# Decode attention on one core: how the first half of the first K is loaded

## The chip, the cores and the metric

The kernel runs on one core of one Trainium2 chip. The metric is the device time of the launch in microseconds (us). Each kernel was timed against the kernel before on the same chip.

## The reference, cut to what matters

One query per head attends to 8192 keys, for 16 heads of width 256:

```python
B, H, Sq, Sk, D = 1, 16, 1, 8192, 256          # q, k, v in bf16
scores = einsum("bhqd,bhkd->bhqk", q, k) * D ** -0.5
out = einsum("bhqk,bhkd->bhqd", softmax(scores), v)
```

K and V are 64 MiB each and each byte is used once. 134.2 MB have to be read from device memory (134.23 in the trace of before); there is little arithmetic per byte.

## The kernel before

A head's K is laid out as 128 partitions of 64 keys ("columns"), 32 KB per partition, and comes in two halves of 32 columns. A half is normally one load of 2 MB: 128 rows of 16 KB. In the traces each row of a load is one packet: before has 9344 data packets, as many as rows (512 of 2 KB, 512 of 4 KB, 640 of 8 KB, 7680 of 16 KB). About 16 packets are under way at a time (exactly 16 for 278 of 318 us), and the page counts 16 DMA engines; what is given per engine below is a sum over packets divided by 16. There are four buffers for halves of K and four for halves of V. The half of K with number n is used by VectorE (columns 0 to 23, one fused multiply-and-sum per column, 0.346 us from one start to the next: 12 of them from 9.30 to 13.45 us in before) and by TensorE (columns 24 to 31). When both are done with it, its buffer takes half n + 4.

All loads are issued in one order by one queue: K halves 0, 1, 2, 3; then K4, V0, K5, V1 and so on. K4 has to wait until K0 has been used, and nothing behind it in this order is issued earlier (V0 followed K4 at 14.26 us in before).

```python
def cuts(kind, n):                       # widths of the loads of one half, in columns
    if kind == "k" and n == 0:
        return FIRST_CUT                 # (4, 4, 8, 16): rows of 2, 2, 4 and 8 KB
    if kind == "v" and n == NIT - 1:
        return LAST_CUT
    if kind == "v" and n in (NIT - 3, NIT - 2):
        return BEFORE_CUT
    return (HALF,)                       # 32 columns: rows of 16 KB
...
for kind, h, x in items:                 # the loads, in the order above
    ...
    if n >= slots:
        waits = [f"{kind}free{n - slots}"] + ([f"ktfree{n - slots}"] if kind == "k" else [])
    for i, wd in enumerate(cuts(kind, n)):
        plan.op("sp", lambda e, ...: e.dma_start(
            b[:, at * D : (at + wd) * D], cols(t, h, c + at, c + at + wd)), ...)
        at += wd
...
# VectorE: one instruction per column, waiting for the load that holds this column
plan.op("dve", lambda e, ...: e.tensor_tensor_reduce(...), name,
        [f"qbc{h}", ring] + landed("k", n, c, c + 1))
```

The cut of K0 into four loads lets VectorE start on the first four columns early (at 4.09 us, see below).

## Time and profile before

| | |
|---|---|
| time, median of the first 3 runs | 324.47 us (324.17 to 325.11) |
| span of the profiled run | 323.3 us |
| data read | 134.2 MB, 415 GB/s over the span |
| VectorE busy | 275.6 us (85%) |
| DMA share | 9 tenths or more in 38 of 40 slices |

Two lines of the page of the kernel before: the DMA share in tenths and the GB/s moved, in 40 equal slices of the span (8.1 us each).

```profile
DMA  7999999999999999999999999999999999999993
GB/s 230 431 438 423 424 430 432 426 424 424 431 432 428 424 432 428 432 426 426 434 430 428 424 428 432 430 430 421 428 432 430 430 423 434 426 428 430 416 417 142
```

From 1.72 us, where the first data packet starts, to 320.05 us, where the last one ends, some data packet is under way at all times but 2 ns. Apart from the last slice, which holds the tail, only the first is slow. The next table, by stages of the kernel before, has the stretch in us, its length, the busy time of PE, PEld, DVE, ACT and POOL with instruction counts, the granted clock, the DMA share and GB/s.

```profile
2.00:8.00 6.00, 1.34 (x6) 0.46 (x6) 2.85 (x16) 1.59 (x6) 0.54 (x5) 1.00 0.91 298
8.00:20.00 12.00, 7.59 (x76) 5.48 (x76) 10.37 (x59) 5.99 (x10) 0.00 (x0) 1.00 1.02 436
50.00:300.00 250.00, 179.67 (x1794) 125.72 (x1791) 228.12 (x1315) 73.69 (x144) 0.00 (x0) 0.87 1.01 428
```

From 2 to 8 us the engines are 91% busy and yet move 298 GB/s; later they move 428. So the share of busy time doesn't say here that the stream is at its rate: read the two columns together.

VectorE's first instruction, and the two later ones in the first 16 us that waited for K (timeline of the kernel before: start, length, engine, line, operation, and in brackets the idle time before it with what ended it):

```profile
4.09 0.42 DVE L359 CUSTOM_DVE_ANT_0 prod<-Kb,qbc 128x256 bf16<-128x256 bf16 x1 [4.09 <-ACT qbc L421]
...
8.06 0.43 DVE L359 CUSTOM_DVE_ANT_0 prod<-Kb,qbc 128x256 bf16<-128x256 bf16 x1 [1.11 <-DMA Kb<-in_k_dram]
...
15.44 0.42 DVE L359 CUSTOM_DVE_ANT_0 prod<-Kb,qbc 128x256 bf16<-128x256 bf16 x1 [1.57 <-DMA Kb<-in_k_dram]
```

The third is the start of the second half of K. VectorE's last instruction on K0 ended at 13.86 us, and the issuing queue then sent K4:

```profile
13.89 0.33 SPq L318 DMA_DIRECT2D Kb<-in_k_dram  x1
```

Last, who VectorE waited for in the whole run (total us, times, longest), and the end of the chain of waits (start, length, what):

```profile
DVE prod L359 <- DMA Kb<-in_k_dram: 22.9, 20, 1.6
```

```profile
306.89 12.36 DMA Vb<-in_v_dram
319.29 1.92 PE acc L604 x16
321.24 0.46 ACT o L618
```

The run ends as the last V loads land, and 4 us after that. So the time is set by when the DMA stream finishes: its start, its rate and any gap in it.

### The profile page before, as it was taken

What the parts mean: (1) busy time and instruction counts of PE and PEld (TensorE: products, weight loads), DVE (VectorE), ACT (ScalarE), POOL (GpSimd) and SP (SyncE); (2) the same over time, 40 slices, a digit from 0 to 9 for tenths busy, and PEclk for the clock granted to TensorE, in tenths of its full rate; (3) what the DMA queues carried; (4) which work ended last, traced back from release to release, by engine and by line L of the source; (5) the groups of instructions that cost most, each with busy time, mean ns of one, the idle gap of its engine ahead of it and who ended that gap; (6) DMA issues with size and microseconds to landing.
All of it is one profiled execution on the core that took longest, in us unless ns stands there. A gap on an engine that the chain in (4) does not pass through costs nothing.

```text
span 323.3 us, 6446 instructions
## 1 busy us (share of the span) xinstructions
PE 223.0 (69%) x2166; PEld 155.7 (48%) x2166; DVE 275.6 (85%) x1586; ACT 94.1 (29%) x185; POOL 1.9 (1%) x12
## 2 busy tenths in 40 slices
PE   1557068783968767685876658676667956858897
PEld 0335045562656545453554535454444644535574
DVE  3899999999999999988889988889888889888600
ACT  3455032422141423323213242312422223232010
POOL 2000000000000000000000000000000000000000
PEclk9999999998697979789778987977887797898799
DMA  7999999999999999999999999999999999999993
GB/s 230 431 438 423 424 430 432 426 424 424 431 432 428 424 432 428 432 426 426 434 430 428 424 428 432 430 430 421 428 432 430 430 423 434 426 428 430 416 417 142
DMA packets 10558, 134.36 MB, mean 416 GB/s; under 512 B 1186, under 2 KB 1203, under 8 KB 2228
## 3 DMA queue, kind: packets, MB, share of 16 engines
q1 hardware_dynamic: 10512, 134.22, 98.2%
q8 instruction: 5, 0.08, 0.1%
q14 instruction: 5, 0.04, 0.0%
q10 hardware_dynamic: 36, 0.02, 0.0%
HBM read 134.23 MB, written 0.01 MB: 415 GB/s over the span
## 4 chain that ended last, share of the span: by engine, by line
DMA 56%; DVE 38%; PE 2%; issue 2%; SPq 1%; DVEq 0%; ACT 0%
DMA Kb<-in_k_dram 41%; DVE prod L359 36%; DMA Vb<-in_v_dram 15%; PE acc L604 2%; DVE S L359 1%; SPq L318 1%; DVE g L331 0%; DVE recip L340 0%; ACT o L618 0%; DVE m L378 0%; DVEq L150 0%; DVEq L147 0%; DVEq L144 0%
## 5 line engine op out<-in xcount | busy, mean ns | idle before, releaser
L359 DVE CUSTOM_DVE_ANT_0 prod<-Kb,qbc 128x256 bf16<-128x256 bf16 x768 | 269.4, 411 | 28.9 <-DMA Kb<-in_k_dram 22.9
L604 PE MATMUL acc<-Vb,E 128*1 128x256 bf16 x1024 | 148.2, 315 | 9.4 <-DMA Vb<-in_v_dram 9.0
L604 PEld LDWEIGHTS acc<-Vb,E 128*1 128x1 bf16 x1024 | 96.5, 96 | 53.5 <-DMA Vb<-in_v_dram 10.7
L499 ACT ACTIVATE KT<-tp 128x1024 bf16<-128x1024 bf16 x64 | 62.0, 1021 | 117.2 <-PE tp L490 117.2
L359 DVE DVE_READ_ACCUMULATOR2_ANT S<- 128x1 f32 x768 | 56.9, 74 | 0.0
L490 PE MATMUL tp<-identb,Kb 128*128 128x128 bf16 x512 | 38.2, 234 | 9.0 <-DMA Kb<-in_k_dram 8.9
L490 PEld LDWEIGHTS tp<-identb,Kb 128*128 128x128 bf16 x512 | 32.3, 105 | 17.1 <-issue 14.4
L516 PE MATMUL spe<-qcur,KT 128*128 128x1 bf16 x512 | 20.6, 165 | 19.6 <-ACT KT L499 19.6
L555 PE MATMUL misc<-g,ones_row 1*128 1x1 f32 x32 | 7.1, 287 | 36.7 <-DVE g L331 36.7
L516 PEld LDWEIGHTS spe<-qcur,KT 128*128 128x128 bf16 x512 | 16.4, 99 | 24.5 <-ACT KT L499 24.3
L618 ACT ACTIVATE o<-acc,recip 1x256 bf16<-1x256 f32 x16 | 7.4, 464 | 71.2 <-PE acc L604 71.2
L555 PEld LDWEIGHTS misc<-g,ones_row 1*128 1x128 f32 x32 | 5.7, 221 | 39.7 <-DVE g L331 39.5
L544 PE MATMUL misc<-ident,m 128*1 128x128 f32 x34 | 7.1, 293 | 15.6 <-DVE m L378 15.6
L544 PEld LDWEIGHTS misc<-ident,m 128*1 128x1 f32 x34 | 1.9, 82 | 19.2 <-DVE m L378 18.8
L562 ACT ACTIVATE negb<-misc 128x1 f32<-128x1 f32 x16 | 2.7, 171 | 27.1 <-PE misc L555 27.1
L331 DVE TENSOR_REDUCE g<-misc 1x1 f32<-1x128 f32 x17 | 4.7, 274 | 5.2 <-PE misc L544 5.2
L584 PE MATMUL misc<-ones_col,lsum 128*1 128x1 f32 x34 | 3.2, 164 | 3.7 <-ACT E L569 3.7
L569 ACT ACTIVATE E<-S,negb 128x64 bf16<-128x64 f32 x16 | 5.6, 348 | 0.7 <-ACT negb L562 0.2
L340 DVE RECIPROCAL recip<-misc 1x1 f32<-1x1 f32 x17 | 2.6, 151 | 3.7 <-PE misc L584 3.7
L438 ACT ACTIVATE qbc<-qb 128x256 bf16<-128x256 bf16 x14 | 5.6, 400 | 0.0
L529 ACT ACTIVATE S<-spe 128x16 f32<-128x16 f32 x16 | 2.9, 183 | 7.2 <-PE spe L516 7.2
L412 PE MATMUL tp<-q,identb 16*128 16x256 bf16 x15 | 4.2, 406 | 1.0 <-ACT qb L421 0.5
(25 smaller groups left out, 21.8 us busy)
## 6 DMA issues: line engine op xcount, KB each, us to landing
Kb<-in_k_dram SPq DMA_DIRECT2D x31, 2048.0 KB, 28.6
Vb<-in_v_dram SPq DMA_DIRECT2D x29, 2048.0 KB, 32.5
Vb<-in_v_dram SPq DMA_DIRECT2D x4, 1024.0 KB, 21.1
Vb<-in_v_dram SPq DMA_DIRECT2D x3, 512.0 KB, 11.6
Kb<-in_k_dram SPq DMA_DIRECT2D x1, 1024.0 KB, 8.3
Kb<-in_k_dram SPq DMA_DIRECT2D x2, 256.0 KB, 3.0
Kb<-in_k_dram SPq DMA_DIRECT2D x1, 512.0 KB, 6.3
Vb<-in_v_dram SPq DMA_DIRECT2D x2, 256.0 KB, 12.6
```

The costliest lines, as they stand in the source:

```text
L331: lambda e: e.tensor_reduce(g[0:1, s : s + 1], misc[s][0:1, MT0 : MT0 + P], AX.X, ALU.max),
L359: lambda e, slot=slot, c=c, col=col, h=h, r=(ttr - 1) % PROD: e.tensor_tensor_reduce(out=prod[:, r * D : (r + 1) * D], in0=Kb[slot][:, c * ...
L412: lambda e, i=i, src=src: e.matmul(bank[:, i * D : (i + 1) * D], lhsT=src[0], rhs=src[1], start=True, stop=True),
L438: lambda e: e.activation(out=qbc[:, s * D : (s + 1) * D], in_=qb[:, (h - 2) * D : (h - 1) * D], func=ACT.Copy),
L490: lambda e, c=c, hf=hf, i=(b * NH + hf) * P, view=view: e.transpose(view[:, i : i + P], Kb[slot][:, c * D + hf * P : c * D + (hf + 1) * P] ...
L499: lambda e, gn=gn, view=view: e.activation(out=KT[gn % KT_SLOTS][:, :], in_=view[:, 0 : GROUP * D], func=ACT.Copy),
L516: lambda e, b=b, hf=hf, oc=oc, gn=gn: e.matmul(spe[sl(h)][:, oc : oc + 1], lhsT=KT[gn % KT_SLOTS][:, (b * NH + hf) * P : (b * NH + hf + 1) ...
L544: lambda e: e.matmul(misc[s][0:1, MT0 : MT0 + P], lhsT=m[:, s : s + 1], rhs=ident[:, :], start=True, stop=True),
L555: lambda e: e.matmul(misc[s][:, BC0 : BC0 + 1], lhsT=ones_row[0:1, :], rhs=g[0:1, s : s + 1], start=True, stop=True),
L569: lambda e: e.activation(out=E[:, s * J : (s + 1) * J], in_=S[:, s * J : (s + 1) * J], func=ACT.Exp, bias=negb[:, h : h + 1], scale=SCALE, ...
L604: lambda e, c=c, col=col: e.matmul(a[0:1, 0:D], lhsT=E[:, col : col + 1], rhs=Vb[slot][:, c * D : (c + 1) * D], start=(x == 0 and c == 0), ...
L618: lambda e: e.activation(out=o[0:1, h * D : (h + 1) * D], in_=acc[s][0:1, 0:D], func=ACT.Copy, scale=recip[0:1, s : s + 1],),
```

## The change

The intent is to make the first load like all others: no short rows and three loads fewer, at the price of a later start of VectorE. The diff is one line:

```diff
-FIRST_CUT = (4, 4, 8, 16)
+FIRST_CUT = (32,)
```

The compute instructions stay the same, apart from three semaphores that VectorE and TensorE no longer wait for; the issuing queue has three loads fewer.

## The prediction

> **What bounds the kernel now.** The DMA stream. On the page the DMA share is 9 from the second slice to the last but one; the table by stages gives 428 GB/s from 50 to 300 us. 134.2 MB at that rate are 314 of the span's 323.3 us; the rest is start-up, a slow stretch at the beginning, and 4 us of tail after the last load of V. VectorE is second (275.6 us, 85%): a half of K costs it 24 x 0.346 + 0.3 = 8.6 us, while the DMA needs 9.8 us for a half of K and one of V. The groups show only 22.9 us of VectorE waits for K.
>
> **The slow stretch.** From 2 to 8 us, when the four small loads run, the DMA moves 298 GB/s although its engines are 91% busy; from 8 to 20 us it moves 436. The missing 130 GB/s over 6 us are 0.8 MB, or 1.8 us at full rate. [...] Some of the loss may be the ramp of a cold stream, which stays.
>
> **What changes.** Removed: three DMA issues, the short rows, and three semaphores that VectorE tests again at every fourth half of K. Added: VectorE can't start on the first 8 columns at 4.09 us; it waits for 2 MB. With data from about 1.9 us on, 4.9 us for 2.1 MB at full rate, and about 2 us from last byte to landing (now 4.2 MB are through at 13.4 us and the second half of K is usable at 15.4), I estimate VectorE's first instruction at 8.5 to 9 us. Without its present waits (1.1 us at 8 us, 1.6 us before the second half of K) it then runs through: first half done at about 17.3 us instead of 13.9, second half begun then instead of at 15.4. So VectorE is 2 us late, not 4.5.
>
> **How much is critical.** The fifth load of K waits for the first buffer; it would be issued at about 17.5 us instead of 14.2. By then about 6.7 of the first 8.4 MB have moved: 4 us of queued work are left, no gap in the DMA, and from then on each 8.6 us of VectorE free 9.8 us of DMA work, so the reserve grows. VectorE's lag of 2 us is absorbed where it has caught up with the loads (after about 110 us it waits for K, 1.2 us per half). What stays is the DMA's gain at the start: I count 1.2 of the 1.8 us. The tail does not change.
>
> **Predicted: 323.2 us, range 321.8 to 324.9.** Faster by over 2%: 0.01; within 2%: 0.97; slower by over 2%: 0.02.
>
> **What would show it.** Right: 2 to 8 us over 380 GB/s; VectorE's first instruction at 8 to 9.5 us; its second half of K begun at 16.5 to 18 us; DMA share 9 to the end; the last V landing about 1 us before today's 319.3 us; the chain ending in V loads as before. Wrong: a dip in GB/s between 15 and 35 us (the queue ran dry, the fifth load issued too late), or VectorE never waiting for K later, so that its 2 us go through to the end.
>
> **What would make it wrong.** The ramp, not the row size, may cause the low rate; then the gain is about 0. [...]

The sum: 1.2 us off the 324.47 us of before, put down as 323.2.

## The result, and the profile after

| | before | after |
|---|---|---|
| median | 324.72 us (6 runs, 324.17 to 325.11) | 323.13 us (6 runs, 323.10 to 323.21) |
| span of the profiled run | 323.3 us | 321.3 us |

The ratio is 0.9952, with a 95% interval of 0.9939 to 0.9965: 0.5% faster. (A ratio here is the mean time of one kernel's fast runs over that of the other's of the same rounds, so it isn't quite the ratio of the medians.) A second timing on another occasion gave 323.17 against 324.42 us, ratio 0.9959. The gain is thus 1.3 to 1.6 us.

The kernel after, the same lines. First the page's slices:

```profile
DMA  7999999999999999999999999999999999999994
GB/s 306 434 430 423 428 426 426 426 434 422 425 430 426 430 428 428 430 426 428 430 428 426 428 430 428 426 428 430 427 426 428 430 425 428 432 426 428 416 417 171
```

The first slice moves 306 instead of 230 GB/s; then the two kernels are alike. The table by stages:

```profile
2.00:8.00 6.00, 1.33 (x6) 0.46 (x6) 0.00 (x0) 1.60 (x6) 0.55 (x5) 1.00 0.90 377
8.00:20.00 12.00, 8.43 (x79) 5.65 (x80) 10.94 (x64) 6.92 (x11) 0.00 (x0) 1.00 1.00 427
50.00:300.00 250.00, 181.67 (x1811) 127.77 (x1809) 232.04 (x1339) 73.69 (x144) 0.00 (x0) 0.87 1.01 428
```

Over the first 20 us the two runs average 352 and 379 GB/s. That is 0.54 MB, or 1.3 us at 428 GB/s. Counting the data packets in the two traces (the bytes of a packet spread evenly over its time) shows when this lead arises and that it stays:

```
MB moved so far                      2.1    8.3    40     100    130    134
after reaches it earlier, by us      1.38   1.42   1.39   1.37   1.36   1.47
```

The whole lead is there after the first 2.1 MB, which is exactly K0. Nothing later adds to it or takes from it, except some 0.5 us in the very last packets of this pair of traces (the last one ends at 320.05 us before and at 318.06 after), where the profiled run of before also happened to be 0.35 us above its median.

VectorE's first instruction in the kernel after, the first one of the second half, and the issue of K4:

```profile
9.06 0.42 DVE L359 CUSTOM_DVE_ANT_0 prod<-Kb,qbc 128x256 bf16<-128x256 bf16 x1 [9.06 <-DMA Kb<-in_k_dram]
...
17.57 0.41 DVE L359 CUSTOM_DVE_ANT_0 prod<-Kb,qbc 128x256 bf16<-128x256 bf16 x1
```

```profile
17.66 0.33 SPq L318 DMA_DIRECT2D Kb<-in_k_dram  x1
```

VectorE starts 5.0 us later and, having no wait between, begins the second half 2.1 us later. K4 is issued 3.8 us later. The GB/s of the slices after that show no dip, so none of it reached the stream. VectorE's waits and the end of the chain:

```profile
DVE prod L359 <- DMA Kb<-in_k_dram: 24.7, 15, 9.1
```

```profile
304.67 12.60 DMA Vb<-in_v_dram
...
317.31 1.92 PE acc L604 x16
...
319.26 0.47 ACT o L618
```

VectorE waited 9.1 us for K0, and 15.6 us in all the rest; before, it waited 22.9 us in pieces of at most 1.6. The chain ends in the same V loads, now 2.0 us earlier in these two traces.

### The profile page after: what moved, and what is told of

The parts are those of the page before. It is cut to its first block, busy times and chain, and to the rows that moved or that the text cites. A ratio compares the mean times of both kernels' runs of the same rounds, so it can differ in the third digit from the quotient of the medians.

```text
span 321.3 us, 6420 instructions
## 1 busy us (share of the span) xinstructions
PE 221.4 (69%) x2166; PEld 155.5 (48%) x2166; DVE 275.2 (86%) x1586; ACT 94.1 (29%) x185; POOL 1.9 (1%) x12
## 4 chain that ended last, share of the span: by engine, by line
DVE 46%; DMA 46%; PE 4%; issue 2%; SPq 0%; DVEq 0%; ACT 0%
DVE prod L359 44%; DMA Vb<-in_v_dram 25%; DMA Kb<-in_k_dram 21%; PE acc L604 4%; DVE S L359 2%; DVE g L331 0%; SPq L318 0%; DVE recip L340 0%; DVEq L150 0%; DVE m L378 0%; ACT o L618 0%; DVEq L147 0%; DVEq L144 0%
## 5 line engine op out<-in xcount | busy, mean ns | idle before, releaser
L604 PE MATMUL acc<-Vb,E 128*1 128x256 bf16 x1024 | 146.0, 312 | 9.8 <-DMA Vb<-in_v_dram 9.8
L604 PEld LDWEIGHTS acc<-Vb,E 128*1 128x1 bf16 x1024 | 95.4, 95 | 52.7 <-DMA Vb<-in_v_dram 11.0
L490 PE MATMUL tp<-identb,Kb 128*128 128x128 bf16 x512 | 39.0, 237 | 6.0 <-DMA Kb<-in_k_dram 6.0
L490 PEld LDWEIGHTS tp<-identb,Kb 128*128 128x128 bf16 x512 | 33.1, 107 | 14.4 <-issue 10.1
```

The source lines that it names most:

```text
L490: lambda e, c=c, hf=hf, i=(b * NH + hf) * P, view=view: e.transpose(view[:, i : i + P], Kb[slot][:, c * D + hf * P : c * D + (hf + 1) * P] ...
L604: lambda e, c=c, col=col: e.matmul(a[0:1, 0:D], lhsT=E[:, col : col + 1], rhs=Vb[slot][:, c * D : (c + 1) * D], start=(x == 0 and c == 0), ...
```

## The experiments

The theory after the result had two parts. A: the four first loads, in the form that they have, slow the stream at its cold start (the first microseconds after the DMA engines were idle), and the change gains what they lost. B: VectorE's later start costs nothing, because K4 is still issued before the queue of loads runs dry. Rivals were: VectorE disturbs the loads by reading while they land; the number of loads costs; short rows are slow anywhere; the addresses of short rows collide.

### VectorE held back under the old loads (e_gate)

```diff
 def landed(kind, n, c0, c1):
     names, at = [], 0
+    if kind == "k" and n % K_SLOTS == 0:
+        c0, c1 = 0, HALF                # every column of K0 waits for all four loads
```

> The four small loads of before, but VectorE and TensorE wait for all four (VectorE begins at about 10.6 us, second half of K at about 19). Theory A (the loads' own form slows the stream; VectorE's start is off the critical path): 2 to 8 us still at about 300 GB/s, time as before, 324.7 us within 0.5. Rival B (VectorE reading K while it lands slows the stream): 2 to 8 us rises to about 380 GB/s and the time falls to about 323.2. Rival C (VectorE's lag goes through to the end): about 328 us.

Measured: 324.55 us (4 runs, 324.51 to 325.10) against 324.93; ratio 0.9991, interval 0.9956 to 1.0026. VectorE's first instruction and the stage of 2 to 8 us in this run:

```profile
10.79 0.42 DVE L361 CUSTOM_DVE_ANT_0 prod<-Kb,qbc 128x256 bf16<-128x256 bf16 x1 [10.79 <-DMA Kb<-in_k_dram]
```

```profile
2.00:8.00 6.00, 1.33 (x6) 0.45 (x6) 0.00 (x0) 1.60 (x6) 0.53 (x5) 1.00 0.99 345
```

VectorE starts 6.7 us later than before and K4 is issued at 19.39 us instead of 13.89, and the time doesn't change by more than the noise of about 1 us: part B holds, and rival C of this expectation falls. The rate of 345 GB/s lies between the two forecasts. It comes from one trace each, and the rate varies between traces of this cut (298 GB/s in before, 292 in e_skew below); the time, which is the better witness, stays with before. So VectorE's reading is not the main cause. A small part of it isn't excluded by this run; e_cut8 below settles it further.

### Four loads of full rows (e_part4)

```diff
-e.dma_start(b[:, at*D:(at+wd)*D], cols(t, h, c + at, c + at + wd))
+e.dma_start(b[32*i:32*i+32, :], cols(t, h, 0, HALF)[32*i:32*i+32, :])   # K0 only, i = 0..3
```

(All of K0 is waited for, by the edit of e_gate.)

> The first half of K in four loads again, but each of 32 partitions with rows of 16 KB; everything waits for all four. If the number of loads and their completions cost the time: as before, 324.7 us, 2 to 8 us near 300 GB/s. If the short rows (or their narrow address range) do: as after, 323.1 us within 0.4, 2 to 8 us near 380 GB/s.

Measured: 327.81 us, ratio 1.0085 (1.0050 to 1.0119): slower than before by almost 3 us, which neither theory had foreseen. Two stages of this run:

```profile
2.00:8.00 6.00, 1.34 (x6) 0.46 (x6) 0.00 (x0) 1.61 (x6) 0.53 (x5) 1.00 0.96 209
8.00:14.00 6.00, 0.57 (x6) 0.60 (x7) 0.53 (x3) 0.00 (x0) 0.00 (x0) 1.00 0.96 253
```

The stream ran at about half its rate until K0 was through at about 12 us: 209 GB/s from 2 to 8 us against 428 later, and K0's packets of 16 KB took 1.26 us (median) instead of 0.61. Not the first packets alone are slow (from 8 to 12 us the stream still moved only 147 to 254 GB/s), and this is the only run whose loads span 32 partitions instead of 128; whether and why that halves the rate was not tested. So this experiment most likely introduced a fault of its own (the author's estimate, from these figures), and says nothing of the number of loads. It does say that this load is better split by columns (324.93 us) than by partitions (327.81 us).

### The rows of a load moved apart in memory (e_skew)

```diff
+def skewed(t, at, wd):
+    pitch = J * D + 128                 # 32 KB + 256 bytes from row to row
+    flat = t[0].rearrange("h s d -> (h s d)")[at * D : at * D + P * pitch]
+    return flat.rearrange("(p r) -> p r", p=P)[:, 0 : wd * D]
```

> The four loads of before with the same rows of 2 to 8 KB, but row p is read 256 bytes times p further on in memory, so that the 128 rows of a load no longer begin at the same address modulo 32 KB. Head 0 is wrong on purpose. If short rows are slow in themselves: 2 to 8 us near 300 GB/s, 324.7 us. If the stall comes from all rows of a load hitting the same narrow address range: 2 to 8 us near 380 GB/s or above and about 323.2 us.

Measured: 324.83 us, ratio 0.9993 (0.9956 to 1.0030).

```profile
2.00:8.00 6.00, 1.34 (x6) 0.46 (x6) 3.17 (x17) 1.61 (x6) 0.54 (x5) 1.00 0.92 292
```

Nothing changed, so the narrow address range modulo 32 KB is not the cause. Only one other address pattern was tried (e_contig below).

### The same cut one half later (e_k1)

```diff
-    if kind == "k" and n == 0:
+    if kind == "k" and n == 1:
         return FIRST_CUT
```

(`landed` is moved from K0 to K1 in the same way.)

> The first half of K whole, the second half cut into the four loads (4, 4, 8, 16). If short rows are slow wherever they stand: about 1.4 us lost at 7 to 12 us, time 324.5. If only a cold start in step makes them slow: the four loads run at nearly full rate (over 400 GB/s from 8 to 14 us) and the time is within 0.4 us of after, 323.1 to 323.5.

Measured: 323.28 us (323.18 to 323.72), ratio 0.9951 (0.9916 to 0.9986). That is the time of the kernel after, though the four loads with rows of 2 to 8 KB are all there. They run between 7 and 12 us here:

```profile
2.00:8.00 6.00, 1.33 (x6) 0.45 (x6) 0.00 (x0) 1.60 (x6) 0.53 (x5) 1.00 0.88 361
8.00:14.00 6.00, 3.77 (x38) 2.72 (x38) 5.10 (x30) 2.48 (x4) 0.00 (x0) 1.00 1.06 442
```

So neither the short rows nor the number of loads costs more than about 0.2 us once the stream is running here (by the count of packets this run is 0.2 us behind after at 40 MB). The loss of before comes with the cold start.

### One first load, but in pieces of 2 KB (e_blocks)

```diff
-b[:, at*D:(at+wd)*D], cols(t, h, c + at, c + at + wd)
+b[:, :].rearrange("p (j r) -> p j r", j=8),                                   # K0 only
+cols(t, h, 0, J).rearrange("p (j i r) -> p j i r", j=8, i=2)[:, :, 0, :],     # every second 2 KB
```

> The kernel after, but its one first load takes 8 pieces of 2 KB per row that are not adjacent in memory, so one load of 2 MB all in 2 KB packets (head 0 is wrong on purpose). A 2 KB packet took 84 ns in the cut kernels, eight of them 672 ns against 611 for one of 16 KB: that alone costs about 0.5 us. If stalls at the cold start come from short packets as such: 2 to 8 us near 300 GB/s and 324.5 us or more. If they come from several loads in a row: no stalls beyond those of after, 323.5 to 323.8 us.

Measured: 325.40 us (325.21 to 325.50), ratio 1.0040 (1.0021 to 1.0058): slower than before.

```profile
2.00:8.00 6.00, 1.34 (x6) 0.46 (x6) 0.00 (x0) 1.59 (x6) 0.54 (x5) 1.00 0.91 246
```

One load, 2 MB, and the stall is there and larger. So 2 KB pieces at a cold start are enough for it; neither several loads nor small ones are needed. Not all of this run's loss is stall. By the count of packets it is 2.1 us behind after at 2.1 MB: 1.05 us of that are stalled packets, about 0.45 us the plain time of eight packets of 2 KB instead of one of 16, and 0.44 us a later first packet (2.16 us instead of 1.72).

### Two loads of 8 KB rows, four loads of 4 KB rows (e_cut16, e_cut8)

```diff
-FIRST_CUT = (4, 4, 8, 16)
+FIRST_CUT = (16, 16)         # e_cut16
+FIRST_CUT = (8, 8, 8, 8)     # e_cut8
```

> The first half of K in two loads of 1 MB with rows of 8 KB. If packet length decides: [...]323.2 to 323.4. If a load's turn at the cold start costs a fixed amount each: one third of the loss of before, about 323.6. VectorE begins at about 6 us.

> The first half of K in four loads of 512 KB with rows of 4 KB: the number of loads of before, but no row of 2 KB. If the number of loads decides: as before, 324.6 to 324.9. If packet length decides: between, about 323.7 to 324.0.

Measured: e_cut16 322.92 us (322.87 to 322.99), ratio 0.9966 (0.9948 to 0.9983); e_cut8 323.10 us (323.04 to 323.22), ratio 0.9971 (0.9953 to 0.9989). Both forecasts of size were too pessimistic. The first instruction of VectorE and the stage of 2 to 8 us in e_cut16, then both in e_cut8:

```profile
5.62 0.42 DVE L359 CUSTOM_DVE_ANT_0 prod<-Kb,qbc 128x256 bf16<-128x256 bf16 x1 [5.62 <-DMA Kb<-in_k_dram]
```

```profile
2.00:8.00 6.00, 1.34 (x6) 0.46 (x6) 2.38 (x13) 1.61 (x6) 0.54 (x5) 1.00 1.00 406
```

```profile
4.45 0.42 DVE L359 CUSTOM_DVE_ANT_0 prod<-Kb,qbc 128x256 bf16<-128x256 bf16 x1 [4.45 <-ACT qbc L421]
...
2.00:8.00 6.00, 1.34 (x6) 0.46 (x6) 3.55 (x21) 1.61 (x6) 0.54 (x5) 1.00 1.01 399
```

Four loads of 512 KB with rows of 4 KB are as good as one of 2 MB (on another chip). They are as many loads and as many rows, 512, as in before, so neither number is the cause; what hurt came with the 2 KB rows. This decides the question of number that e_part4 had left open. It also answers the rival about VectorE: here VectorE reads K0 from 4.45 us on, while the rest of K0 is landing, and the stream runs at 399 GB/s all the same.

### 2 KB rows behind a first load of 4 KB rows (e_mid4)

```diff
-FIRST_CUT = (4, 4, 8, 16)
+FIRST_CUT = (8, 4, 4, 16)
```

> The four loads of before in another order: first 8 columns (rows of 4 KB), then 4 and 4 (2 KB), then 16 (8 KB). If 2 KB rows are slow only while the stream is cold: no stalls beyond the first packets, 2 to 8 us near 390 GB/s, 323.1 to 323.5. If they are slow anywhere in the first 5 us or so: as before, 2 to 8 us near 310 GB/s, about 324.5.

Measured: 323.92 us (323.51 to 324.41), ratio 0.9983 (0.9957 to 1.0008).

```profile
2.00:8.00 6.00, 1.33 (x6) 0.45 (x6) 3.43 (x19) 1.61 (x6) 0.54 (x5) 1.00 0.97 339
```

It lies between: about half of the loss is back. All four runs are above all six of after on the same chip (at most 323.31), while the interval doesn't separate it from before. With 0.5 MB ahead of the 2 KB rows part of the loss remained (323.92 us); with 2 MB ahead of them (e_k1, 323.28 us) it was gone. The durations of single data packets in the traces, for packets begun in the first 15 us, show where the time goes:

```
           2 KB packets         4 KB packets         8 KB packets         16 KB packets
           mean / longest, us   mean / longest       mean / longest       mean / longest
before     0.106 / 0.62         0.188 / 1.31         0.396 / 1.48         0.616 / 0.79
e_gate     0.095 / 0.50         0.205 / 0.95         0.349 / 1.49         0.620 / 0.79
e_blocks   0.110 / 1.30         -                    -                    0.612 / 0.64
e_mid4     0.087 / 0.59         0.222 / 1.05         0.386 / 1.42         0.612 / 0.63
e_cut8     -                    0.175 / 0.88         -                    0.611 / 0.62
e_cut16    -                    -                    0.340 / 1.01         0.611 / 0.62
after      -                    -                    -                    0.641 / 1.48
e_k1       0.084 / 0.12         0.159 / 0.17         0.309 / 0.32         0.653 / 1.42
```

The row of e_k1 is what a packet of 2 to 8 KB takes in a running stream (one of 16 KB takes 0.61 us there; the mean in this row holds the program's first packets). In every kernel of the table the very first packets are stalled (longest 0.50 to 1.48 us); in after, e_cut8 and e_cut16 that is nearly all. In before, e_gate and e_mid4 the packets of 4 and 8 KB that come with or behind the 2 KB rows are stalled too, up to 1.5 us each; in e_mid4 those of 2 KB hardly are (0.087).

The packets also say what the 1.38 us of lead after K0 are made of, per DMA engine: 0.65 us is the difference in stalled packets (time above the row of e_k1, for 16 KB above 0.61; 1.28 us in before and 0.63 in after), 0.2 us is what short rows take in a running stream too, and 0.5 us is time in which engines had no packet at all, between 3.5 and 6 us. This last part shows in the three runs that begin with the old cut (before 0.54 us, e_skew 0.49, e_gate 0.21) and not in e_mid4 or e_cut8. Where it comes from was not settled, nor whether a mixture of row lengths at the start does harm of its own: no run mixes lengths without having rows of 2 KB.

### All loads unbroken in memory (e_contig)

```diff
-return t[0, h].rearrange("(p j) d -> p (j d)", p=P)[:, c0*D : c1*D]
+return t[0, h].rearrange("(x p j) d -> x p (j d)", p=P, x=2)[c0 // HALF][:, c0 % HALF * D : (c1 - 1) % HALF * D + D]
```

> The kernel after with the keys of a half laid out so that every load is one unbroken 2 MB of memory (rows of 16 KB that follow each other; keys and values are permuted alike, the result stays right). The stream runs at 0.61 us per 16 KB packet on each engine[...], so no change in the steady rate, 428 GB/s. If the first packets' stall (1.3 us each instead of 0.61) comes from the 32 KB distance between rows, it goes away and the time falls by up to 0.6 us to 322.5; else 323.1.

Measured: 323.43 us (323.33 to 323.64), ratio 0.9983 (0.9965 to 1.0001), 358 GB/s from 2 to 8 us; the longest 16 KB packet of the first 15 us took 1.73 us. No gain: the stall of the first packets isn't due to the distance of 32 KB between rows.

### VectorE delayed until the queue runs dry (e_late24)

```diff
+for i in range(24):                     # before VectorE's first instruction on K0
+    dve(lambda e, i=i: e.tensor_tensor_reduce(out=dum[...], in0=Kb[0][...], ...),
+        f"late{i}", ["qbc0"] + landed("k", 0, 0, 1))
```

> The kernel after with 24 extra VectorE instructions (8.3 us) before its first, after the first half of K has landed. The fifth load of K is issued at about 26.0 us instead of 17.7; the 8.4 MB queued before it are through at about 21.9 us and its first data come 0.9 us after issue, so the DMA should stand still for about 5.0 us and the time should be about 328.1 us (327.5 to 328.7). If VectorE's lag went through in full: 331.4. If it were absorbed in full: 323.1.

Measured: 334.14 us (333.59 to 335.18), ratio 1.0309 (1.0282 to 1.0336): 11.0 us slower than after on the same chip (323.17), much more than expected. The timeline of the issuing queue, VectorE at its first proper instruction, and the stages around the gap:

```profile
31.21 0.33 SPq L321 DMA_DIRECT2D Kb<-in_k_dram  x1
```

```profile
22.61 0.43 DVE L377 CUSTOM_DVE_ANT_0 prod<-Kb,qbc 128x256 bf16<-128x256 bf16 x1 [6.05 <-issue]
```

```profile
20.00:22.00 2.00, 0.00 (x0) 0.00 (x0) 0.00 (x0) 0.00 (x0) 0.00 (x0) 1.00 0.91 381
22.00:32.00 10.00, 4.54 (x42) 3.05 (x43) 9.39 (x54) 3.80 (x7) 0.00 (x0) 1.00 0.01 6
32.00:34.00 2.00, 1.74 (x8) 0.45 (x6) 2.00 (x13) 1.53 (x5) 0.00 (x0) 1.00 0.94 254
```

The model held and one input was wrong. The extra instructions took their 8.3 us, but VectorE then stood still for another 6.05 us with nothing that the profile shows to wait for. So K4 was issued at 31.2 us, not at 26.0. The queued loads ended at about 22 us and the DMA was idle for 10 us. Put into the sum that the expectation used, 31.2 + 0.9 - 21.9 gives 10.2 us; the spans differ by 331.8 - 321.4 = 10.4 us. K4 was 13.55 us later than in after, and 10.4 of them reached the end: the reserve of the kernel after is about 3 us of delay. The restart shows something else: after 10 us without work the first 16 packets of 16 KB took 1.26 us on average, as at the start of the program (1.18 us in after), and the later ones 0.61. So the stall of the first packets comes after a pause too, not at the start of the program alone. Why VectorE stood still was not settled. The trace has 8 KB packets of the instruction queue at 19.0 and 20.5 us, in that gap, and 7 such packets instead of 5 in the whole run; whether they have to do with the gap was not tested.

### A version that beats both, side by side (after_again, e_best)

> The kernel after once more, unchanged, on the chip on which the two-load version is timed: 323.1 us.

> The two loads of 1 MB once more, beside the kernel after on the same chip. It had 322.92 us elsewhere, with the DMA's last packet 0.3 us earlier than in after. If that is real, 0.1 to 0.3 us below after; if it was the other chip, no difference.

Measured on one chip, six runs each: after 323.17 us (322.86 to 323.31), the two loads of 1 MB 322.92 us (322.84 to 322.96), ratios to before 0.9959 and 0.9952. The means are 323.15 and 322.92 us. The two-load form is 0.2 us (0.07%) faster, and had the same median, 322.92 us, in both timings. It is tiny, but only one of the six runs of after (322.86) lies within the range of the two-load form. In its trace the DMA leads after by 0.1 us when the first 2.1 MB are through, and its last packet ends 0.25 us earlier (317.81 against 318.06 us). Whether VectorE's earlier start has a part in it is not shown: e_gate's interval is wider than 0.2 us.

## Why the prediction was right, point by point

- **The DMA stream bounds the kernel, and VectorE's start is off the critical path.** Right. VectorE began at 9.06 us (predicted 8.5 to 9), the second half at 17.57 (17.3), K4 was issued at 17.66 (17.5), and no dip followed. e_gate shows it by itself: VectorE 6.7 us later, no change in time beyond the noise. VectorE did catch up, though later than the 110 us that were named: its regular waits for K of over 1 us begin at 139 us before and at 176 us after.
- **The gain is the loss of the first 6 us, less a part that stays.** Right in mechanism and size: 1.2 us were predicted and 1.3 to 1.6 us measured. The size was partly luck: how the 1.8 us divide into 1.2 gained and 0.6 kept was not worked out, and the range reached up to no gain at all. The rate from 2 to 8 us was 377 GB/s, just under the 380 that were named, for the first packets are stalled in after too (0.63 us per engine): the ramp that stays.
- **A lead at the start is kept to the end.** Right: 1.38 us after K0, 1.36 us at 130 MB.
- **What the slow stretch comes from.** The prediction named the small loads and the short rows together. The runs separate them: four loads of 512 KB lose nothing (e_cut8, 323.10 us), one load of 2 MB in 2 KB pieces loses the most of these (e_blocks, 325.40 us), and the original four loads lose at most 0.2 us behind a running stream (e_k1, 323.28 us). The one larger load was faster here, but size was not the reason.
- **The reserve.** Estimated at 4 us of queued work; e_late24 gives about 3 us of further delay. The difference fits the time from issue to data, which the estimate had left out: the author put it at 0.9 us, and in e_late24 K4 was issued at 31.21 us and no data packet began between 24 and 32.
- **What stays open:** why 2 KB rows stall a cold stream, also for the longer rows behind them (up to 1.48 us for 8 KB in before); why engines stood without a packet for 0.5 us in before; why 2 MB of head start cured it (e_k1, 323.28 us) and 0.5 MB didn't (e_mid4, 323.92 us); and why the loads of 32 partitions ran at 209 GB/s (e_part4).

## What to carry to other kernels

Where a stream of loads bounds a kernel, as here, judge a finer first cut by what it does to the stream, not by how early the compute starts: here 5 us of earlier start were worth nothing that could be measured, and 1.3 to 1.6 us of lost stream went straight to the end. Cutting the first load was harmless here as long as its rows stayed at 4 KB or more (two loads of 8 KB rows, 322.92 us; four of 4 KB rows, 323.10 us; one load, 323.13 to 323.17 us) and each load spanned all 128 partitions (four loads of 32 took 327.81 us). The late consumer cost nothing that could be measured as long as the load that waits for its buffer was issued before the queue was empty (K4 at 17.66 us in after, at 19.39 us in e_gate); in the one run that went beyond that point (e_late24, K4 at 31.21 us), what exceeded the reserve of about 3 us came out at the end.
